# The front of a fused scan and two-layer MoE kernel in another order, its loads a block sooner, and its narrow exponentials in one operation

## The chip, the cores and the metric

The kernel runs on one core of a Trainium2 chip. The metric is the device time of one execution in microseconds, from the median of several runs. A core has five engines with a queue of instructions each: TensorE (PE in the profile; PEld is its loading of weights), VectorE (DVE), ScalarE (ACT), GpSimd (POOL), and SyncE (SP), which here issues nearly all DMAs.

## The reference

A chunked linear scan (4 sequences, 8 heads, 768 steps, head width 32, state width 16) feeds two feed-forward layers.

```python
log_a = np.log(np.clip(a, 1e-06, 1.0))
for c in range(nc):                        # chunks of 32 steps
    cum = np.cumsum(la, axis=-1)
    L = np.exp(cum[:, :, :, None] - cum[:, :, None, :]) * causal
    M = np.einsum('bhin,bhjn->bhij', Cc, Bc) * L
    y = np.einsum('bhij,bhjd->bhid', M, xc) + np.einsum('bhin,bhnd->bhid', Cc, state) * np.exp(cum)
    state = np.exp(np.sum(la, axis=-1)) * state + np.sum(Bx, axis=2)   # Bx: B x decayed to the chunk's end
x = y reshaped to [3072, 256]
h = np.maximum(np.maximum(x @ w1, x @ w2), x @ w3)        # 256 -> 768, three matrices
x = h @ w_out                                              # 768 -> 256
h = x @ w_in                                               # 256 -> 2048
out = (np.maximum(h, 0) + alpha * np.minimum(h, 0)) @ v_out    # 2048 -> 256
```

The weights arrive as 64-bit floats.

## The kernel before

The tokens are cut into 24 blocks of 128 steps (`r`; four sequences of six) for the scan and into 6 tiles of 512 tokens for the two layers. Blocks 0 to 8 are narrow: each is two chunks of 64 steps, and its mask-and-decay tile `e` (`blk[r]["m"]`) is 128 x 8 heads x 64. Blocks 9 to 23 are wide.

A block passes through steps with these names: `load_bc` and `load_x` (its B, C and x; narrow blocks from 2 on also load B and C turned, `bt` and `ct`), `cum_rows` (its rows of summed logs, broadcast from a tensor `cum_d` in DRAM into `e`; and `cpt`), `att_a` (B and C times decays, `bp` and `cp`, on GpSimd, L370), `att_t` (turned B and C, spread over heads), `att_e` (the exponential of `e` plus a column of negated log sums, one ACT operation for each head, L477, then two masks on GpSimd, L480), `att_b` (C times B on TensorE, L499, times `e` on VectorE, L504), `att_u` (the new state) and `att_y` (the output, L573 and L581, copied into the token tile `xt`, L590 and L591). Blocks 0 and 1 don't read `cum_d`: `first_e` makes their `e` by a matmul with the triangle (L455, L459, L461) and one exponential of 128x512 (L463). `sums(half)` adds up the logs of half the steps, writes them to `cum_d` (L295) and makes the decay columns (L300 to L306).

The weights come in 28 pieces of 512 KB. `fetch_weights` starts a piece's load into one of three buffers; `convert` turns it into two fp32r parts, high and low, in four steps, of which `next_weights(n)` emits the next n: a shift on VectorE (L178), a merge on VectorE (L180), the fetch of a later piece and the high part on ScalarE (L184), the low part on VectorE (L186) with ScalarE's rescaling of the next piece (L171). Matmuls of the layers are three products of high and low parts each (`parts`, L775); `halves` makes the high and low part of an activation (ACT L138, then L139, mostly on GpSimd).

The order around the change is written out by hand in the front (L1115 to L1168): warm-up matmuls (`idle`, L1110, on a cleared tile `warm`), the logs, the first loads, blocks 0 and 1 with 16 conversion steps between. Then phase 0 begins, the first layer on tile 0, cut into halves of 256 tokens: its first four units need blocks 0 and 1, the fifth blocks 2 and 3 as well. In phase 0 a planner that works with estimated times chooses the order on each engine; units, scan steps (`todo`) and conversion steps are emitted in turn. From phase 1 on the written order holds. `load(r)` (L221) loads a block's B, C and x; with `AHEAD = 8`, from block 8 on it loads the next block's B and C.

Each engine works its queue strictly in order, SyncE's DMA issues too.

Of the kernel before, what the change touches and what calls it, by code (L numbers as in the profile page):

```python
# [9 lines left out]
F32 = mybir.dt.float32  # L10
F32R = mybir.dt.float32r
BF16 = mybir.dt.bfloat16
U32 = mybir.dt.uint32
I64 = mybir.dt.int64
AF = mybir.ActivationFunctionType
ALU = mybir.AluOpType
# [3 lines left out]
P = 128  # L20
BT, H, S, D, N = 4, 8, 768, 32, 16
DM = H * D
NB = S // P
Q = 64
# [18 lines left out]
LEADW = 12288  # L43

STRICT = 1
AHEAD = 8
START = 4

FINE = 6
# [11 lines left out]
WARM = 8  # L61
# [23 lines left out]
def fused(ctx: ExitStack, tc: tile.TileContext, x, a, B, C, Bt, Ct, w1, w2, w3, w_out, v_in, v_out, alpha, cst, out):  # L85
    nc = tc.nc

    def pool(name, bufs, **kw):
        return ctx.enter_context(tc.tile_pool(name=name, bufs=bufs, **kw))
# [1 line left out]
    const = pool("const", 1)  # L91
    wts = pool("wts", 1)
    stage = pool("stage", 2)
    ld = pool("ld", 2)
    sm = pool("sm", 2)
    stk = pool("stk", 1)
    NDIR = BW * NB + KW
# [10 lines left out]
    def ptile(p, tag, shape=(P, 512)):  # L108
        return p.tile(list(shape), F32, tag=tag, name=tag)

    ct = const.tile([P, C_N], F32, name="ct")
# [11 lines left out]
    ncum = const.tile([P, NB, BT, H], F32, name="ncum")  # L123
# [6 lines left out]
    def st_tile():  # L130
        return stage.tile([P, 1024], U32, tag="st", name="st", bufs=3)
# [24 lines left out]
    def words(i):  # L156
        w = staged[i].rearrange("p (f w) -> p f w", w=2)
        return w[:, :, 0], w[:, :, 1]

    def fetch_weights():  # L160
        i = len(staged)
        if i < len(wq):
            st = st_tile()
            nc.sync.dma_start(st.bitcast(I64).rearrange("p (k f) -> p k f", k=2), wq[i][1])
            staged.append(st)

    def rebias(i):


        hi = words(i)[1].bitcast(F32)  # L170
        nc.scalar.activation(hi, hi, AF.Prelu, scale=2.0 ** -112, alpha=2.0 ** 32)  # L171
# [29 lines left out]
    def next_weights(n):  # L201
        for _ in range(n):
            done[0] += 1
            next(steps, None)
# [16 lines left out]
    def load(r):  # L221
        for q in (r, r + 1)[r > AHEAD:1 + (r >= AHEAD)]:
            load_bc(q)
        load_x(r)

    def load_bc(r):
        if r >= NR:
            return
        b, k = divmod(r, NB)
        s = slice(k * P, (k + 1) * P)  # L230
        d = blk.setdefault(r, {})
        direct = NPA <= r < NDIR
        for nm, src in (("b", B), ("bt", Bt), ("ct", Ct)) if direct else (("b", B), ("c", C)):
            if nm[1:]:
                t = d[nm] = ld.tile([P, P], F32, tag=nm, name=nm)
                nc.sync.dma_start(t, src[b, :, :, s].rearrange("h n t -> (h n) t"))
            else:
                t = d[nm] = ld.tile([P, H, N], F32, tag=nm, name=nm)
                nc.sync.dma_start(t, src[b, s])

    def load_x(r):
        if r >= NR:
            return
        b, k = divmod(r, NB)
        d = blk.setdefault(r, {})
        d["x"] = xm[r % NX]
        if r >= NDIR:
            d["x"] = xm[r % NX][:, 0]
            nc.sync.dma_start(d["x"], x[b, k * P:(k + 1) * P])
            return  # L250
        for c in range(2):
            s = slice(k * P + c * Q, k * P + (c + 1) * Q)
            nc.sync.dma_start(d["x"][c * Q:(c + 1) * Q, c], x[b, s])
# [9 lines left out]
    warm = un.tile([P, 512], F32, tag="g", name="g")[:, :256].bitcast(BF16)  # L263
# [131 lines left out]
    def att_t(r, part=None):  # L395
        d = blk[r]
        if r >= NDIR:
            ts = sm.tile([P, 7 * P], F32, tag="ts", name="ts", bufs=1)
            used = 6 + (r % NB > 0)
            nc.vector.transpose(ts[:, :6 * P], tok[0].bitcast(F32).rearrange("p s c -> p (s c)"))  # L400
            if used > 6:
                nc.vector.transpose(ts[:, 6 * P:], d["cp"].rearrange("p h n -> p (h n)"))
            sc = d["sc"] = dr.tile([7, P, P], F32, tag="sc", name="sc")
            for i in range(4):
                o = slice(32 * i, 32 * i + 32)
                nc.sync.dma_start(sc[:used, :, o].rearrange("s (v q) t -> q (s v) t", v=4), ts[o, :used * P].rearrange("q (w t) -> q w t", t=32))
            return
        if r >= NPA:
            bt, ct_, cpt = d["bt"], d["ct"], d["cpt"]
            bc = stk.tile([P, 6, P], F32R, tag="bc", name="bc").bitcast(F32)  # L410
            bs, cs = d["bs"], d["cs"] = bc[:, :2], bc[:, 2:4]
            nc.scalar.activation(cpt, cpt, AF.Exp)
            for i in range(2):
                nc.scalar.activation(cs[:, i, :], ct_, AF.Copy, scale=par[i])
            nc.vector.tensor_tensor(bs, bt.unsqueeze(1).to_broadcast([P, 2, P]), pairs.to_broadcast([P, 2, P]), ALU.mult)
            nc.gpsimd.tensor_tensor(cpt, ct_, cpt, ALU.mult)
            return
        keys = [("b", "c"), ("cp",)][part]
        pt = ptile(ps_acc, "acc", (P, 3, P))
        for i, key in enumerate(keys):  # L420
            nc.tensor.transpose(pt[:, i, :], d[key].rearrange("p h n -> p (h n)"), ident)
        if "cp" in keys:
            cpt = d["cpt"] = sm.tile([P, P], F32, tag="cpt", name="cpt")
            nc.scalar.activation(cpt, pt[:, len(keys) - 1, :], AF.Copy)
        if "b" in keys:
            bc = stk.tile([P, 6, P], F32R, tag="bc", name="bc").bitcast(F32)
            bs, cs = d["bs"], d["cs"] = bc[:, :2], bc[:, 2:4]
            for i in range(2):
                nc.scalar.activation(cs[:, i, :], pt[:, 1, :], AF.Copy, scale=par[i])
            nc.vector.tensor_tensor(bs, pt[:, 0:1, :].to_broadcast([P, 2, P]), pairs.to_broadcast([P, 2, P]), ALU.mult)  # L430
# [35 lines left out]
    def att_e(r, part=None):  # L466
        b, k = divmod(r, NB)
        if r >= NDIR:
            for g in range(2) if part is None else (part,):
                e = blk[r]["m", g]  # L470
                for q in range(4):
                    nc.scalar.activation(e[:, q, :], e[:, q, :], AF.Exp, bias=ncum[:, k, b, 4 * g + q:4 * g + q + 1])  # L472
                nc.gpsimd.affine_select(out=e, in_=e, pattern=[[0, 4], [1, P]], compare_op=ALU.is_ge, fill=0.0, base=0, channel_multiplier=-1)  # L473
            return
        e = blk[r]["m"]
        for h in range(4 * (part or 0), 4 if part == 0 else H):
            nc.scalar.activation(e[:, h, :], e[:, h, :], AF.Exp, bias=ncum[:, k, b, h:h + 1])  # L477
        for c in range(0 if part == 0 else 2):
            m = e[c * Q:(c + 1) * Q]
            nc.gpsimd.affine_select(out=m, in_=m, pattern=[[0, H], [1, Q]], compare_op=ALU.is_ge, fill=0.0, base=0, channel_multiplier=-1)  # L480

# [625 lines left out]

    junk = ps_up.tile([P, 512], F32, tag="up", name="up")

    def idle(n):  # L1110

        for _ in range(n):
            nc.tensor.matmul(junk, warm[:, :P], warm, start=True, stop=True, skip_group_check=True)  # L1113

    with tc.manual_schedule():  # L1115
        for t in xm:
            nc.gpsimd.memset(t, 0.0)
        nc.vector.memset(warm, 0.0)
        idle(WARM)
        logs()  # L1120
        load_bc(0)
        fetch_weights()
        nc.sync.dma_start(s_c[:BT * H, C_SEL:], cst[:BT * H, C_N + C_SEL:])
        load_x(0)
        fetch_weights()
        load_bc(1)
        load_x(1)
        fetch_weights()
        cum_rows(0)
        cum_rows(1)  # L1130
        su, e0, e1 = sums(0), first_e(0), first_e(1)
        next(e0)
        next(e1)
        att_t(0, 0)
        next(e0)
        back()
        att_a(0, "bp")
        next(su)
        next(e0)
        next(su)  # L1140
        rebias(0)
        next_weights(1)
        next(e1)
        next(e0)
        next(su)
        next_weights(2)
        next(su)
        att_a(0, "cp")
        att_a(1)
        next_weights(1)  # L1150
        att_b(0)
        next_weights(2)
        next(e1)
        att_u(0)
        next(e1)
        att_t(0, 1)
        att_t(1, 0)
        att_t(1, 1)
        next_weights(1)
        att_y(0)  # L1160
        next_weights(1)
        att_b(1)
        att_u(1)
        idle(IDLE)
        next_weights(3)
        att_y(1)
        next_weights(1)
        next_weights(START)  # L1168
    load(2)
    if True:  # L1170
        nc.sync.dma_start(alph, alpha.rearrange("(k p) -> p k", p=P))
        todo += [(go, 0) for go in (
# [23 lines left out]
        for n_ph, ph in enumerate(PHASES):  # L1196
# [5 lines left out]
            layer, t, _, pace = ph  # L1202
# [62 lines left out]
```

## Time and profile before

| | |
|---|---|
| median of 3 runs | 537.24 us (536.43 to 538.32) |
| the profiled execution | 538.03 us, of which the span from the first to the last instruction 536.3 |
| mean granted TensorE clock | 0.997 of full speed |
| TensorE busy | 524.7 us (98%), 3382 matmuls |
| VectorE, ScalarE, GpSimd busy | 326.9, 261.4, 243.8 us |
| chain that ended last | TensorE 88%, VectorE 4%, ScalarE 2%, issue 2%, GpSimd 1%, DMA 1% |

Times in the profile are microseconds from the span's start. A row of a timeline gives start, length, engine, line and operation, the tile written and those read, shapes and the count; in square brackets stands the idle time of the engine just before and what ended it. Two matmuls overlap in the pipeline, so their lengths add up to more than the time they take. The granted clock is the share of full speed that the chip allowed TensorE.

### The profile page before, as it was taken

Reading aid. Unit: us, or ns where it says so; the run is one execution under the profiler, and the core shown is the slowest. Engines: PE = TensorE matmul, PEld = TensorE weight load, DVE = VectorE, ACT = ScalarE, POOL = GpSimd, SP = SyncE. Lnnn points to the kernel's source line nnn. Section 1 sums busy time; section 2 is a strip of 40 time slices with the busy share of each in tenths; the row PEclk is TensorE's granted clock in tenths of the full one; section 3 lists DMA queues with packets and bytes.
Section 4 is the critical chain, followed back from the end, with each engine's and each line's share of the span. In section 5 each row is a group of like instructions: output and inputs, shape, how many; then the busy total and the mean of one; then the engine's idle time right before and its main releaser. Section 6 shows DMA issues by size and latency. Waiting matters only on the chain.

```text
span 536.3 us, 9516 instructions
## 1 busy us (share of the span) xinstructions
PE 524.7 (98%) x3382; PEld 428.6 (80%) x3382; DVE 326.9 (61%) x566; ACT 261.4 (49%) x612; POOL 243.8 (45%) x267
## 2 busy tenths in 40 slices
PE   8888999999999999999999999999999999999997
PEld 4767887788888888888888888888888888778886
DVE  5895686788573446665447676337665636775453
ACT  6676675666756324333333433423432324766561
POOL 2153354434645324645424655432653352885550
PEclk9998999999999999999999999999999999999999
DMA  7667566487544534423716324633440200000024
GB/s 212 184 187 230 162 177 168 135 228 191 171 112 104 130 99 109 104 78 86 155 44 160 75 82 119 141 82 90 98 99 1 39 0 1 1 2 0 1 40 119
DMA packets 147744, 56.52 MB, mean 105 GB/s; under 512 B 87920, under 2 KB 139568, under 8 KB 147696
## 3 DMA queue, kind: packets, MB, share of 16 engines
q1 hardware_dynamic: 145328, 55.38, 40.0%
q10 hardware_dynamic: 2368, 0.52, 0.4%
q8 instruction: 27, 0.44, 0.4%
q14 instruction: 21, 0.17, 0.1%
HBM read 45.26 MB, written 10.62 MB: 104 GB/s over the span
## 4 chain that ended last, share of the span: by engine, by line
PE 88%; DVE 4%; ACT 2%; issue 2%; SPq 1%; POOL 1%; DMA 1%; ACTq 0%; POOLq 0%; DVEq 0%
PE up L775 47%; PE acc L775 28%; PE at L775 5%; PE at L489 1%; PE at L614 1%; DVE v L180 1%; DMA xm<-in_x_dram 1%; PE at L499 1%; PE at L606 1%; PE up L1113 1%; PE at L581 1%; PE at L573 0%; SPq L295 0%; POOL e L480 0%; ACT e L472 0%
## 5 line engine op out<-in xcount | busy, mean ns | idle before, releaser
L139 POOL TENSOR_TENSOR gl<-g,gh 128x512 fp32r<-128x512 f32 (+1 forms) x109 | 137.2, 1259 | 214.6 <-ACT gh L138 190.2
L775 PE MATMUL up<-xt,w 128*128 128x512 f32 (+1 forms) x777 | 169.2, 365 | 1.8 <-DVE g L801 0.6
L775 PEld LDWEIGHTS up<-xt,w 128*128 128x128 f32 x777 | 133.2, 190 | 27.9 <-issue 2.2
L138 ACT ACTIVATE gh<-g 128x512 fp32r<-128x512 f32 (+1 forms) x114 | 69.4, 609 | 172.0 <-DVE g L820 73.8
L775 PE MATMUL up<-yt,vi 128*128 128x512 f32 x459 | 116.6, 389 | 0.0
L801 DVE TENSOR_TENSOR g<-up,g 128x512 f32<-128x512 f32 (+1 forms) x84 | 51.2, 610 | 82.4 <-PE up L775 79.8
L775 PEld LDWEIGHTS up<-yt,vi 128*128 128x128 f32 x459 | 86.1, 188 | 17.9
L775 PE MATMUL acc<-gh,vo 128*128 128x512 f32 x268 | 83.2, 392 | 0.0
L819 DVE TENSOR_SCALAR g<-up,alph 128x512 f32<-128x512 f32 x48 | 35.9, 749 | 37.7 <-PE up L775 37.7
L775 PEld LDWEIGHTS acc<-gh,vo 128*128 128x128 f32 x268 | 49.6, 188 | 10.2 <-issue 0.2
L775 PE MATMUL acc<-gl,vo 128*128 128x512 f32 x134 | 52.2, 389 | 0.0
L775 PE MATMUL acc<-gh,wo 128*128 128x512 f32 (+1 forms) x168 | 47.4, 364 | 0.4 <-DVE yt L848 0.4
L472 ACT ACTIVATE e<-e,ncum 128x128 f32<-128x128 f32 x120 | 37.9, 388 | 0.0
L799 ACT ACTIVATE g<-up 128x512 f32<-128x512 f32 (+1 forms) x42 | 22.3, 530 | 28.3 <-PE up L775 16.3
L775 PEld LDWEIGHTS acc<-gh,wo 128*128 128x128 f32 x168 | 29.8, 189 | 5.6 <-DVE yt L848 0.5
L820 DVE SCALAR_TENSOR_TENSOR g<-up,g 128x512 f32<-128x512 f32 x48 | 33.2, 691 | 1.6
L775 PE MATMUL acc<-gl,wo 128*128 128x512 f32 (+1 forms) x84 | 30.4, 362 | 0.3 <-POOL gl L139 0.3
L775 PEld LDWEIGHTS acc<-gl,vo 128*128 128x128 f32 x134 | 25.2, 188 | 5.3
L473 POOL TENSOR_SCALAR_AFFINE_SELECT e<-e 128x512 f32<-128x512 f32 x30 | 19.2, 643 | 12.2 <-ACT e L472 12.2
L180 DVE SCALAR_TENSOR_TENSOR v<-st,v 128x512 uint32<-128x512 uint32 x28 | 23.1, 825 | 2.1 <-ACT st L171 1.4
L817 DVE SCALAR_TENSOR_TENSOR g<-g,rest,up 128x512 f32<-128x512 f32 x16 | 11.9, 743 | 15.0 <-ACT g L816 14.8
L1002 DVE SCALAR_TENSOR_TENSOR g<-g,rest,up 128x512 f32<-128x512 f32 x16 | 12.0, 747 | 11.9 <-ACT g L1001 11.6
(199 smaller groups left out, 675.2 us busy)
## 6 DMA issues: line engine op xcount, KB each, us to landing
e<-cum_w SPq DMA_DIRECT2D x30, 256.0 KB
st<-sc SPq DMA_DIRECT2D x60, 128.0 KB
sc<-ts SPq DMA_DIRECT2D x52, 112.0 KB
st<-in_moe_w_out_dram SPq DMA_DIRECT2D x11, 512.0 KB
st<-in_moe_w_dram SPq DMA_DIRECT2D x9, 512.0 KB
st<-in_moe_w_in_dram SPq DMA_DIRECT2D x8, 512.0 KB
v<-sc SPq DMA_DIRECT2D x60, 64.0 KB
out_dram<-st SPq DMA_DIRECT2D x20, 128.0 KB
```

Of the source, the lines that this page charges most:

```text
L138: nc.scalar.activation(dst_h, src, AF.Copy)
L139: engine.tensor_tensor(dst_l, src, dst_h, ALU.subtract)
L180: nc.vector.scalar_tensor_tensor(v, hi, 3, v, ALU.logical_shift_left, ALU.bitwise_or)
L472: nc.scalar.activation(e[:, q, :], e[:, q, :], AF.Exp, bias=ncum[:, k, b, 4 * g + q:4 * g + q + 1])
L473: nc.gpsimd.affine_select(out=e, in_=e, pattern=[[0, 4], [1, P]], compare_op=ALU.is_ge, fill=0.0, base=0, channel_multiplier=-1)
L775: nc.tensor.matmul(acc, w, r, start=(first and i == 0), stop=(last and i == len(todo_) - 1), skip_group_check=True)
L799: nc.scalar.activation(g, p, AF.Copy)
L801: nc.vector.tensor_tensor(g, p, g, ALU.max)
L817: nc.vector.scalar_tensor_tensor(g, g, rest[:, f:f + 1], p, ALU.mult, ALU.add)
L819: nc.vector.tensor_scalar(g, p, 0.0, alph[:, f:f + 1], ALU.min, ALU.mult)
L820: nc.vector.scalar_tensor_tensor(g, p, 0.0, g, ALU.max, ALU.add)
L1002: nc.vector.scalar_tensor_tensor(g, g, rest[:, f:f + 1], h, ALU.mult, ALU.add)
```

## The change

The front is emitted in another order: the g of block 0 ahead of its `att_t`, block 0's `att_b`, `att_u` and block 1's `att_t` sooner, two conversion steps later, the third piece's fetch ahead of block 1's x, and the loads of block 2 and of block 3's B and C in the front. `load(r)` loads the next block's B and C from block 3 on (`AHEAD = 2`). The buffers of B, C and turned C become three, turned C shares those of C; turned B keeps two. The narrow blocks' `att_e` adds the column of log sums by one GpSimd operation and then takes one exponential over all heads. The warm-up matmuls read a constant that is there from the start.

```diff
-AHEAD = 8
+AHEAD = 2
...
-    ld = pool("ld", 2)
+    ld = pool("ld", 3)
...
             if nm[1:]:
-                t = d[nm] = ld.tile([P, P], F32, tag=nm, name=nm)
+                tag, bufs = ("c", 3) if nm == "ct" else ("bt", 2)
+                t = d[nm] = ld.tile([P, P], F32, tag=tag, name=nm, bufs=bufs)
...
         e = blk[r]["m"]
-        for h in range(4 * (part or 0), 4 if part == 0 else H):
-            nc.scalar.activation(e[:, h, :], e[:, h, :], AF.Exp, bias=ncum[:, k, b, h:h + 1])
-        for c in range(0 if part == 0 else 2):
+        if part != 1:
+            nc.gpsimd.tensor_tensor(e, e, ncum[:, k, b, :].unsqueeze(2).to_broadcast([P, H, Q]), ALU.add)
+        if part == 0:
+            return
+        nc.scalar.activation(e, e, AF.Exp)
+        for c in range(2):
             m = e[c * Q:(c + 1) * Q]
...
-    def idle(n):
-
+    def idle(n, early=False):
+
+        w = nc.const_aps.tensor(1.0, [P, 512], BF16) if early else warm
         for _ in range(n):
-            nc.tensor.matmul(junk, warm[:, :P], warm, start=True, stop=True, skip_group_check=True)
+            nc.tensor.matmul(junk, w[:, :P], w, start=True, stop=True, skip_group_check=True)
...
-        idle(WARM)
+        idle(WARM, True)
         logs()
         load_bc(0)
         fetch_weights()
...
         load_x(0)
         fetch_weights()
         load_bc(1)
+        fetch_weights()
         load_x(1)
-        fetch_weights()
+        load_bc(2)
         cum_rows(0)
         cum_rows(1)
         su, e0, e1 = sums(0), first_e(0), first_e(1)
         next(e0)
         next(e1)
+        next(e0)
         att_t(0, 0)
-        next(e0)
         back()
         att_a(0, "bp")
         next(su)
         next(e0)
         next(su)
+        next(e0)
         rebias(0)
         next_weights(1)
+        att_b(0)
+        next(su)
+        next_weights(1)
         next(e1)
-        next(e0)
+        att_u(0)
+        next_weights(1)
+        load_x(2)
+        att_t(1, 0)
         next(su)
-        next_weights(2)
-        next(su)
+        next(e1)
         att_a(0, "cp")
         att_a(1)
         next_weights(1)
-        att_b(0)
-        next_weights(2)
         next(e1)
-        att_u(0)
-        next(e1)
+        next_weights(1)
         att_t(0, 1)
-        att_t(1, 0)
+        att_b(1)
+        next_weights(1)
         att_t(1, 1)
-        next_weights(1)
         att_y(0)
         next_weights(1)
-        att_b(1)
         att_u(1)
+        next_weights(2)
         idle(IDLE)
+        att_y(1)
+        load_bc(3)
         next_weights(3)
-        att_y(1)
-        next_weights(1)
         next_weights(START)
-    load(2)
```

## Rows read from the trace of the kernel before

**Rows 1.** Windows: length; PE, PEld, DVE, ACT, POOL busy; PEclk; DMA share; GB/s.
```profile
20.00:38.00 18.00, 17.14 (x189) 14.16 (x189) 16.59 (x39) 13.32 (x41) 6.53 (x9) 1.00 0.75 198
38.00:42.00 4.00, 1.93 (x24) 1.65 (x24) 2.30 (x7) 2.85 (x10) 3.23 (x6) 1.00 0.49 118
42.00:48.00 6.00, 6.00 (x82) 5.14 (x79) 3.20 (x10) 4.02 (x14) 2.17 (x4) 0.72 0.66 193
48.00:100.00 52.00, 50.77 (x590) 42.40 (x588) 36.55 (x85) 35.87 (x108) 23.42 (x33) 1.00 0.62 180
100.00:520.00 420.00, 419.80 (x2241) 345.14 (x2241) 250.09 (x387) 190.77 (x411) 201.61 (x205) 1.00 0.35 86
```

**Rows 2.** Waits of PE from 0 to 120 us: total, times, longest.
```profile
PE at L573 <- DVE e L504: 1.4, 1, 1.4
...
PE at L573 <- POOL cpt L416: 0.7, 1, 0.7
```

**Rows 3.** Timeline of the front, 0 to 24 us.
```profile
1.25 3.59 PE L1113 MATMUL up<-g 128*128 128x512 bf16 x8 [1.25 <-DVE g L1118]
...
3.45 0.84 ACT L272 ACTIVATE xt<-xt 32x768 f32<-32x768 f32 x1 [1.37 <-DVE xt L271]
...
8.39 1.12 PE L461 MATMUL up<-g,yt 128*128 128x512 f32 x2 [0.86 <-DVE g L459]
...
9.55 0.69 DVE L459 TENSOR_TENSOR g<-scr 128x512 f32<-128x512 f32 x1 [0.35 <-PE up L461]
...
10.64 0.85 PE L499 MATMUL at<-bc 64*64 64x128 f32 x16
...
12.59 0.60 ACT L463 ACTIVATE e<-up 128x512 f32<-128x512 f32 x1 [0.24 <-PE up L461]
...
16.40 0.75 DVE L504 TENSOR_TENSOR e<-at,e 128x256 f32<-128x256 f32 x2
...
17.38 0.60 DVE L544 SCALAR_TENSOR_TENSOR u<-u,dec_f 128x64 f32<-128x64 f32 x2
...
18.11 0.65 PE L581 MATMUL at<-e,xm 128*32 128x64 f32 x32
18.43 0.69 DVE L180 SCALAR_TENSOR_TENSOR v<-st,v 128x512 uint32<-128x512 uint32 x1
...
19.16 0.63 ACT L184 ACTIVATE w<-v 128x512 fp32r<-128x512 f32 x1 [3.01 <-DVE v L180]
...
20.00 1.93 PE L775 MATMUL up<-xt,w 128*128 128x256 f32 x14 [0.60 <-ACT xt L590]
...
20.39 0.68 DVE L186 TENSOR_TENSOR w<-v,w 128x512 fp32r<-128x512 f32 x1
```

**Rows 4.** Timeline around block 3's exponentials, 24 to 50 us.
```profile
36.50 0.33 ACT L477 ACTIVATE e<-e,ncum 128x64 f32<-128x64 f32 x1
...
37.22 0.79 POOL L139 TENSOR_TENSOR gl<-g,gh 128x256 fp32r<-128x256 f32 x1 [3.92 <-DMA b<-in_B_dram]
...
37.48 1.52 ACT L477 ACTIVATE e<-e,ncum 128x64 f32<-128x64 f32 x6
...
39.71 0.62 POOL L370 TENSOR_TENSOR bp<-b,dec_b 128x128 f32<-128x128 f32 x1
...
40.40 0.66 POOL L480 TENSOR_SCALAR_AFFINE_SELECT e<-e 64x512 f32<-64x512 f32 x1
...
41.66 0.45 PE L573 MATMUL at<-cpt,u 32*64 32x64 f32 x8 [1.40 <-DVE e L504]
```

**Rows 5.** Groups by line and form: count, busy us, mean ns, idle before.
```profile
L477 ACT ACTIVATE e<-e,ncum 128x64 f32<-128x64 f32 x56 | 15.2, 336 | 0.0
...
L139 POOL TENSOR_TENSOR gl<-g,gh 128x512 fp32r<-128x512 f32 x97 | 126.3, 1302 | 192.4 <-ACT gh L138 176.3 <-DMA v<-sc 4.6 <-PE acc L775 4.4
```

**Rows 6.** Timeline, a conversion beside a GpSimd subtraction, 88 to 95 us.
```profile
92.56 1.33 POOL L139 TENSOR_TENSOR gl<-g,gh 128x512 fp32r<-128x512 f32 x1 [2.52 <-ACT gh L138]
...
92.86 1.59 DVE L180 SCALAR_TENSOR_TENSOR v<-st,v 128x512 uint32<-128x512 uint32 x1
```

## The prediction

> **What bounds the kernel now.** I read three views in this order. First the windows: from 100 us to 520 us TensorE is busy for 419.80 of 420 us at full clock [rows 1]. There the reader is to see that no other engine's saving can shorten that part; only what TensorE waits for before it can. The window from 48 to 100 us has 50.77 of 52, so 1.2 us idle. Between 20 and 38 us TensorE is busy 17.14 of 18 while VectorE has 16.59 of 18; between 38 and 42 us TensorE is busy 1.93 of 4; and from 42 to 48 us it is busy all the time, but at a granted clock of 0.72 [rows 1]. Second the waits of TensorE: the two that stand out are block 3's output matmuls (L573), 1.4 us for VectorE's masked product (L504) and 0.7 us for GpSimd's product (L416) [rows 2]. Third the timeline, for why these come late [rows 3, 4].
>
> So the time to win is in four places: the front, up to the first matmul of the weights at 20.00 [rows 3]; idle before 38 us (18 - 17.14 = 0.86); the gap of 38 to 42 us (4 - 1.93 = 2.07); and the fall of the clock behind it, (1 - 0.72) x 6 = 1.68 us [rows 1]. The clock fell right after the gap, and nowhere else in the windows. Together with the 1.2 us between 48 and 100 that is what is there; everything else is TensorE's own work, which the change leaves as it is.
>
> **The front.** *Warm-up.* The eight warm-up matmuls start at 1.25, behind VectorE's clearing of their operand, and take 3.59, to 4.84 [rows 3]. With a constant as operand they can start when the engines do, some 0.4 earlier, and end at 4.44. The logarithm is done at 3.45 + 0.84 = 4.29 [rows 3], so what follows on TensorE starts about 0.35 earlier.
>
> *Block 0 ahead of block 1.* The first L461 began at 8.39 after waiting 0.86 for VectorE [rows 3]; its operand g now goes ahead of att_t's operation, so it can run at 8.39 - 0.35 - 0.86 = 7.2 to 8.3. From there I add up the new order, each step at its row in [rows 3]: CB matmuls 0.85 and their products 0.75; conversion 0.69; g of block 1 0.69; L461 1.12, to 12.4. ScalarE has a weight step of about 0.6 (estimated from the 0.63 of L184) before the exponential of 0.60: 13.6. Block 1's CB matmuls end half a microsecond later; products 0.75; conversion 0.69; about 1.4 for block 0's last VectorE work and block 1's state (0.60 of it L544): 17.0. Then small matmuls, about 0.2, L581 0.65, and a copy of xt. The copy does not have to pass the 0.63 of L184 any more, which stood ahead of it at 19.16. First weight matmul: 18.2 to 18.3 in place of 20.00, a gain of up to 1.7.
>
> *How much of it counts.* The new order does two conversion steps later than the old one: at att_y(1) piece 2 still lacks L180, which ran at 18.43 before. After the front it has L180 0.69, a copy on ScalarE 0.63 and L186 0.68 before it, and starts at about 18.85: it is ready at 20.9, against 20.39 + 0.68 = 21.07 [rows 3]. The third of the three products needs piece 2, so TensorE stops there, with 12 matmuls done, and VectorE then goes on through the same list, busy 16.59 of 18 [rows 1]. The ends are 0.2 (VectorE sets the pace) and 1.7. I take 0.4, near the first, because VectorE is the fuller engine there. The loads of blocks 2 and 3 in the front cost SyncE's queue nothing that I count: no matmul waits for them in the front, and weights that land later by what these bring are used at the end of it. If that cover is gone, the weights behind them land up to 1.6 us later (an estimate: 320 KB of block 2's loads at the 198 GB/s of the window from 20 to 38 us [rows 1]); I take the lower end of this part down to -0.5 for that.
>
> **The exponentials.** Before: eight ACT operations of 336 ns a block, 56 in all, 15.2 us [rows 5]. After: one of 128x512, 0.60 by the form of L463 [rows 3], so 7 x (2.69 - 0.60) = 14.6 us leave ScalarE. GpSimd gets 7 additions of 128x512. No such addition is in the trace; the nearest row is the subtraction L139 of that shape, 1302 ns [rows 5], and I take 1.3 each, 9.1 in all. None of these sums is on the path as such; what counts is block 3.
>
> **Block 3 and the gap.** Its first exponential starts at 36.50; with other work between, the last of six ends at 37.48 + 1.52 = 39.00; then GpSimd masks, but between its two masks stands bp of block 4 (L370, 0.62), and the second ends at 41.06; TensorE waits 1.40 more [rows 4]. Changed: the addition needs cum_d's rows and the log sums alone, GpSimd had nothing to do from 33.3 to the L139 at 37.22 [rows 4], so it is done before. One exponential from 36.5 ends at 37.1. bp of block 4 has its load a block sooner and can go into GpSimd's empty stretch, so the masks (0.66 each) can follow at 37.2 to 38.5, or at 38.0 to 39.4 behind L139 (0.79). Product and small matmuls are then due about 39.3 to 40.2, where TensorE still had weight matmuls up to 40.25 (41.66 - 1.40 = 40.26). That takes away nearly all of the 2.07. The other end is that GpSimd keeps its order: L139, L416, mask, bp, mask in a row from 37.22 end at about 40.6, only 0.5 sooner than 41.06. I take 1.8, as the early load speaks for the first. What is late next is VectorE's conversions, as in the stretch before.
>
> **The clock.** It was 1.00 up to 42 us, with a front as thin as it was, and 0.72 after a gap of this size [rows 1]. With the gap filled I count the whole 1.68 as gained, say 1.7; if more than about half the gap stays, nothing.
>
> **What GpSimd's additions cost VectorE.** L180 took 0.69 with GpSimd idle at 18.43 [rows 3] and 1.59 at 92.86 beside an L139 (92.56 to 93.89) [rows 6]: 0.9 lost to one GpSimd operation of just this shape. Where VectorE has slack that is free. Two additions, of blocks 2 and 3, fall between 18 and 38 us where it has none: 0 to 1.8, I take 0.4, since they meet such an operation for part of their time. The Trainium skill's "GPSIMD Engine Reference" (Specifications) says GpSimd shares its SBUF interfaces with VectorE, in contention with VectorE instructions that have two SBUF inputs; L180 is one, and the trace agrees. The same page (Engine selection) would not put a two-input elementwise operation on GpSimd at all, as about twice as slow.
>
> **Later loads.** From block 3 on each load call issues the same number of transfers as before, B's and C's one block further on; the third buffers are taken from a tag that loses one, so no transfer waits for a tile that it did not wait for. Between 48 and 100 us I count 0 (bounds +1.2, all its idle time, and -1).
>
> **The sum.** 0.4 + 1.8 + 1.7 - 0.4 = 3.5 us. Against the profiled execution's 538.03 (span 536.3, 1.7 around it) that gives 534.5; the median of the three runs is 0.8 lower, 537.24, so the prediction is 533.7.
>
> **Rivals.** A: the whole front counts as well, and the idle 0.86 before 38 us goes: 1.7 + 0.86 + 2.07 + 1.7 = 6.3, so 530.9. For it: the first tile's work then starts with ScalarE free. Against it: piece 2 is no sooner. B: the gap stays. GpSimd keeps its order (0.5 of the gap), TensorE still idles beyond 1 us, the clock falls as before: 0.4 + 0.5 - 0.4 = 0.5, so 536.7. For it: the order of this stretch is a planner's and not the written one. C, slower: GpSimd's additions stretch VectorE's two-input operations. Price 0.9 for each of seven, 6.3 at most; it decides where VectorE is full, in 18 to 38 us (two additions), and in the window after 48 us for those beside conversions, where I count three: 5 x 0.9 = 4.5. The gap then stays too, so 4.5 less the 0.9 of front and gap is +3.6, 540.8. It decides once the additions in the full stretch cost more than the 0.9 that is won there. For it: [rows 6]. Against it: after 48 us VectorE is busy 36.55 of 52 [rows 1], and each narrow block's additions find their rows landed early. This is the outcome to which the skill's sentence on shared interfaces would lead.
>
> **Chances and range.** Forecast 0.46, A 0.20, B 0.20, C 0.14. A measurement of this kernel can tell about 0.3% (1.6 us) from no change. Faster by more than that (below 535.6): the forecast nearly whole, A, and a little of B: 0.67. Within it: most of B and a little of the forecast and C: 0.21. Slower: 0.12. The range goes from A with some of the later idle time, 530.3, to the lower half of C, 538.3.
>
> **What would show it.** Right: the gap of 38 to 42 us is gone from TensorE's windows and the clock stays 1.00 after it; the first L775 is at about 18.3 and its matmuls of the third product wait for L186 till about 21; ACT has 7 exponentials of 128x512; the last GpSimd operation before block 3's product is the second mask, with no bp between. Wrong: the clock still falls somewhere before 60 us; L180's and L186's means grow beside GpSimd's additions; or an L139 stands waiting behind an addition that waits for cum_d. A result above 536 would mean the gap was not what held the end; one below 531 that the front's start counts in full.

## The result, and the profile after

The changed kernel takes 543.50 us in the median of 6 runs (539.86 to 546.12), against 537.25 before: a ratio of 1.0109 (95% interval 1.0080 to 1.0137). Nine more runs gave 541.54 and 1.0068 (1.0042 to 1.0095). It is slower, and the forecast of 533.7 with its range to 538.3 missed it. The profiled execution took 545.8 us, its span is 544.1, 7.8 more than before, and its mean granted clock 0.981.

The windows say where that went. They are those of [rows 1], with three of the changed kernel's own between (columns as there).

```profile
20.00:38.00 18.00, 17.09 (x146) 13.95 (x146) 13.87 (x31) 9.98 (x24) 5.84 (x8) 0.69 0.71 185
27.00:40.50 13.50, 13.00 (x107) 10.63 (x100) 9.42 (x23) 6.92 (x17) 3.84 (x7) 0.50 0.75 195
38.00:42.00 4.00, 4.00 (x26) 4.00 (x26) 2.44 (x6) 1.36 (x3) 0.73 (x1) 0.68 0.69 197
42.00:48.00 6.00, 3.29 (x47) 2.44 (x45) 3.35 (x8) 2.50 (x6) 3.85 (x7) 0.95 0.46 121
44.50:47.00 2.50, 0.48 (x7) 0.28 (x8) 0.91 (x2) 1.38 (x3) 1.69 (x4) 1.00 0.28 89
47.50:54.00 6.50, 5.86 (x76) 4.95 (x76) 4.10 (x9) 1.52 (x4) 1.44 (x3) 0.50 0.51 142
48.00:100.00 52.00, 50.01 (x582) 41.58 (x583) 38.19 (x90) 27.88 (x72) 23.91 (x36) 0.94 0.56 166
100.00:520.00 420.00, 419.46 (x2293) 344.66 (x2292) 249.87 (x387) 191.46 (x419) 200.43 (x206) 1.00 0.35 88
```

The gap did not close: it moved from 38 to 42 us to 44.5 to 47, with 2.50 - 0.48 = 2.02 us idle in place of 2.07. And TensorE now runs at half its clock (granted 0.50: 1.2 GHz in place of 2.4) twice, for 13.7 us and for 6.8 us; the windows from 27.00 and from 47.50 lie inside these two stretches. Before, it was 3.4 us, once. Half of 20.5 us is 10.2 us of full-speed work; before it was 1.7. That difference of 8.5 is more than the whole 7.8. In single runs of this one program the mean clock is between 0.981 and 0.994, and the time goes with it: 545.8, 546.0 and 546.1 at 0.981, 541.1 at 0.991, 539.9 and 541.2 at 0.994. The clock is most of its spread of 6 us, not all: span times clock, which would then be the same in all fifteen runs, lies between 532.8 and 536.5 us.

TensorE's waits up to 120 us, as [rows 2]:

```profile
PE at L577 <- POOL cpt L417: 2.4, 2, 2.0
PE up L779 <- DVE g L805: 1.0, 1, 1.0
PE at L577 <- DVE e L508: 0.8, 1, 0.8
```

The front, as [rows 3], in the profiled execution of the changed kernel (line numbers are 4 or so higher than before):

```profile
0.84 3.57 PE L1118 MATMUL up<-const-bfloat16-1.0 128*128 128x512 bf16 x8 [0.84 <-PEq L1256]
3.56 0.84 ACT L273 ACTIVATE xt<-xt 32x768 f32<-32x768 f32 x1 [1.47 <-DVE xt L272]
8.68 1.70 PE L462 MATMUL up<-g,yt 128*128 128x512 f32 x2
13.09 1.13 PE L462 MATMUL up<-g,yt 128*128 128x512 f32 x2
19.59 1.70 PE L779 MATMUL up<-xt,w 128*128 128x256 f32 x12
```

The warm-up ends at 4.41, as forecast. The first weight matmul comes at 19.59, not at 18.3: the same pair of L462 took 1.70 at 8.68 and 1.13 at 13.09, so the matmuls ran well below full speed until about 10 us. The trace's record of the granted clock begins only at 9.86 us, at full speed; the 1.00 that the windows print before that stands for no entry. The order as written does not decide this: kernel `i2_write_act` below has the same front, its record begins at 3.68, and in its profile

```profile
0.84 3.28 PE L1118 MATMUL up<-const-bfloat16-1.0 128*128 128x512 bf16 x8 [0.84 <-PEq L1256]
6.88 1.12 PE L462 MATMUL up<-g,yt 128*128 128x512 f32 x2
```

and the first L779 at 18.13. What decides it is not shown.

Block 3, which [rows 4] show before, on GpSimd, ScalarE, TensorE and VectorE in the changed kernel:

```profile
33.10 0.40 POOL L371 TENSOR_TENSOR bp<-b,dec_b 128x128 f32<-128x128 f32 x1 [2.18 <-DMA b<-in_B_dram]
41.08 0.73 POOL L139 TENSOR_TENSOR gl<-g,gh 128x256 fp32r<-128x256 f32 x1 [7.57 <-ACT gh L138]
43.26 0.74 POOL L139 TENSOR_TENSOR gl<-g,gh 128x256 fp32r<-128x256 f32 x1 [1.44 <-ACT gh L138]
43.95 1.04 POOL L478 TENSOR_TENSOR e<-e,ncum 128x512 f32<-128x512 f32 x1
45.03 0.63 ACT L481 ACTIVATE e<-e 128x512 f32<-128x512 f32 x1 [0.78 <-POOL e L478]
45.73 0.65 POOL L484 TENSOR_SCALAR_AFFINE_SELECT e<-e 64x512 f32<-64x512 f32 x1 [0.73 <-ACT e L481]
46.36 0.45 POOL L417 TENSOR_TENSOR cpt<-ct,cpt 128x128 f32<-128x128 f32 x1
46.86 0.45 PE L577 MATMUL at<-cpt,u 32*64 32x64 f32 x8 [2.02 <-POOL cpt L417]
47.57 0.76 DVE L508 TENSOR_TENSOR e<-at,e 128x256 f32<-128x256 f32 x2 [2.15 <-POOL e L484]
```

GpSimd stood idle for 7.57 us from 33.5 with the addition of block 3 in its queue: ahead of it were two L139, which wait for TensorE by way of ScalarE, and TensorE ran at half its clock. So the first fall of the clock delays the two L139, these the addition, and that the exponential, the masks and `cpt`; there is the gap, and behind it the clock falls a second time. The fall makes the gap late, but the gap does not need it: `e3_warm_tile` below has the same order on GpSimd and runs at full clock from 15.2 to 42.5 us, and there

```profile
41.48 0.45 PE L577 MATMUL at<-cpt,u 32*64 32x64 f32 x8 [2.02 <-POOL cpt L417]
```

The groups of [rows 5], and a conversion beside an addition for [rows 6]:

```profile
L478 POOL TENSOR_TENSOR e<-e,ncum 128x512 f32<-128x512 f32 x7 | 7.4, 1059 | 6.2 <-DMA e<-cum_d 6.2
L481 ACT ACTIVATE e<-e 128x512 f32<-128x512 f32 x7 | 4.4, 624 | 1.6 <-POOL e L478 1.6
L180 DVE SCALAR_TENSOR_TENSOR v<-st,v 128x512 uint32<-128x512 uint32 x28 | 21.6, 771 | 1.0
```

```profile
75.01 1.04 POOL L478 TENSOR_TENSOR e<-e,ncum 128x512 f32<-128x512 f32 x1
75.47 1.14 DVE L186 TENSOR_TENSOR vi<-v,vi 128x512 fp32r<-128x512 f32 x1
```

An addition took 1.06, less than the 1.3 forecast; L186, 0.68 alone, took 1.14 beside one.

### The profile page after: what moved, and what is told of

The parts are those of the page before. It is cut to its first block, busy times and chain, and to the rows that moved or that the text cites. A ratio compares the mean times of both kernels' runs of the same rounds, so it can differ in the third digit from the quotient of the medians.

```text
span 544.1 us, 9468 instructions
## 1 busy us (share of the span) xinstructions
PE 532.2 (98%) x3382; PEld 433.6 (80%) x3382; DVE 330.8 (61%) x566; ACT 253.0 (46%) x563; POOL 247.7 (46%) x274
## 4 chain that ended last, share of the span: by engine, by line
PE 84%; DVE 5%; issue 4%; POOL 3%; ACT 2%; DMA 1%; ACTq 0%; SPq 0%; POOLq 0%; DVEq 0%
PE up L779 45%; PE acc L779 28%; PE at L779 5%; PE at L493 1%; PE at L618 1%; POOL gl L139 1%; DVE v L180 1%; PE at L585 1%; PE at L610 1%; PE at L577 1%; POOL e L484 1%; DMA e<-cum_d 1%; POOL e L478 1%; DVE v L178 1%; PE at L503 0%
## 5 line engine op out<-in xcount | busy, mean ns | idle before, releaser
L139 POOL TENSOR_TENSOR gl<-g,gh 128x512 fp32r<-128x512 f32 (+1 forms) x109 | 135.9, 1247 | 213.7 <-ACT gh L138 197.1
L779 PE MATMUL up<-xt,w 128*128 128x512 f32 (+1 forms) x777 | 171.2, 369 | 1.7 <-DVE g L805 1.0
L779 PEld LDWEIGHTS up<-xt,w 128*128 128x128 f32 x777 | 135.5, 195 | 27.2 <-issue 1.6
L779 PE MATMUL up<-yt,vi 128*128 128x512 f32 x459 | 116.7, 389 | 0.0
L779 PEld LDWEIGHTS up<-yt,vi 128*128 128x128 f32 x459 | 86.1, 188 | 17.9
L779 PE MATMUL acc<-gh,vo 128*128 128x512 f32 x268 | 83.2, 392 | 0.0
L779 PEld LDWEIGHTS acc<-gh,vo 128*128 128x128 f32 x268 | 49.5, 188 | 10.2 <-issue 0.2
L779 PE MATMUL acc<-gl,vo 128*128 128x512 f32 x134 | 52.2, 389 | 0.0
L779 PE MATMUL acc<-gh,wo 128*128 128x512 f32 (+1 forms) x168 | 48.9, 371 | 0.3 <-DVE yt L852 0.3
L779 PEld LDWEIGHTS acc<-gh,wo 128*128 128x128 f32 x168 | 30.9, 195 | 5.9 <-DVE yt L852 0.5
L779 PE MATMUL acc<-gl,wo 128*128 128x512 f32 (+1 forms) x84 | 30.9, 368 | 0.0
L779 PEld LDWEIGHTS acc<-gl,vo 128*128 128x128 f32 x134 | 25.2, 188 | 5.3
L180 DVE SCALAR_TENSOR_TENSOR v<-st,v 128x512 uint32<-128x512 uint32 x28 | 21.6, 771 | 1.0
```

The lines of the kernel that those rows point to most:

```text
L139: engine.tensor_tensor(dst_l, src, dst_h, ALU.subtract)
L180: nc.vector.scalar_tensor_tensor(v, hi, 3, v, ALU.logical_shift_left, ALU.bitwise_or)
L779: nc.tensor.matmul(acc, w, r, start=(first and i == 0), stop=(last and i == len(todo_) - 1), skip_group_check=True)
```

## The experiments

All timed beside the kernel before. "Lost" is (1 - granted clock) x span, the median over a kernel's runs: what the clock took. The other columns are times in its profiled execution: the end of the issue of the second half sums' write to `cum_d`, the issue of block 3's rows from `cum_d`, the start of block 3's product (L504 before), and the start of VectorE's maximum `g` at about 91 us, explained below. "At 91" and span are given as differences from the kernel before.

| kernel | median us | ratio [95%] | lost | write | rows | product | at 91 | span |
|---|---|---|---|---|---|---|---|---|
| before | 537.2 to 537.9 | 1 | 0.5 to 1.6 | 27.0 | 30.2 | 41.1 | (91.17) | (536.3) |
| changed | 543.50 | 1.0109 [1.0080, 1.0137] | 7.6 | 29.2 | 32.3 | 47.6 | +7.7 | +7.8 |
| `e1_exp_only` | 536.59 | 0.9983 [0.9969, 0.9996] | 0.0 | 27.1 | 30.5 | 39.5 | -2.3 | -2.3 |
| `e2_front_only` | 546.67 | 1.0160 [1.0137, 1.0184] | 8.7 | 28.5 | 31.4 | 45.1 | +8.3 | +8.5 |
| `e3_warm_tile` | 540.82 | 1.0074 [1.0046, 1.0101] | 5.4 | 27.3 | 31.1 | 42.2 | +2.5 | +2.8 |
| `f1_loads_only` | 543.72 | 1.0119 [1.0093, 1.0146] | 6.2 | 27.3 | 30.1 | 42.6 | +6.9 | +6.9 |
| `f2_order_only` | 537.42 | 1.0017 [0.9994, 1.0041] | 2.1 | 27.1 | 30.6 | 38.5 | -0.6 | -0.6 |
| `f3_front_conv` | 544.56 | 1.0126 [1.0096, 1.0156] | 6.8 | 26.8 | 30.1 | 45.8 | +6.5 | +6.6 |
| `f4_exp_loads` | 538.93 | 1.0031 [1.0017, 1.0045] | 2.2 | 28.2 | 31.0 | 42.6 | +0.7 | +1.0 |
| `g1_ahead_only` | 543.55 | 1.0110 [1.0060, 1.0161] | 6.0 | 28.7 | 31.8 | 47.5 | +8.5 | +8.5 |
| `g2_block2_front` | 538.42 | 1.0006 [0.9991, 1.0020] | 1.6 | 23.4 | 29.6 | 41.4 | -0.2 | +0.3 |
| `g3_exp_order` | 538.91 | 1.0014 [0.9993, 1.0035] | 2.4 | 27.7 | 30.5 | 39.0 | -1.5 | -1.4 |
| `g4_filled` | 539.40 | 1.0034 [1.0023, 1.0044] | 1.1 | 27.4 | 30.4 | 41.8 | +0.7 | +0.7 |
| `h1_x_first` | 540.26 | 1.0054 [1.0033, 1.0074] | 3.0 | 28.5 | 31.7 | 43.9 | +1.7 | +2.3 |
| `h2_buffers_only` | 538.20 | 1.0005 [0.9990, 1.0020] | 1.6 | 25.7 | 29.2 | 40.4 | -0.9 | -0.4 |
| `h3_warm_only` | 537.38 | 1.0003 [0.9988, 1.0018] | 1.6 | 26.7 | 30.3 | 41.1 | +0.1 | 0.0 |
| `h4_turned_sooner` | 542.52 | 1.0089 [1.0064, 1.0115] | 4.1 | 28.2 | 31.3 | 43.9 | +4.6 | +4.9 |
| `i2_write_act` | 540.03 | 1.0060 [1.0037, 1.0083] | 4.3 | 24.3 | 30.8 | 41.0 | +1.7 | +1.8 |
| `h6_exp_order_filled` | 537.60 | 1.0028 [0.9999, 1.0057] | 1.1 | 27.6 | 31.6 | 39.3 | -1.2 | -1.2 |

**The exponentials against the front, and the warm-up.** The first three undo a part each. `e1_exp_only` is the kernel before with the new `att_e` alone; `e2_front_only` the changed kernel with the old eight exponentials; `e3_warm_tile` the changed kernel with

```diff
-        idle(WARM, True)
+        idle(WARM)
```

> The kernel before with nothing but the narrow exponentials changed (GpSimd's addition, one exponential). Queue theory: the addition stands in GpSimd's queue behind low-part subtractions that wait for TensorE, so block 3 comes later than before and TensorE's gap at 38 to 42 us grows: 539 to 543 us. Front theory (the written order and the loads are what costs): the same as before or up to 2 us faster, 535 to 537.5.

> The changed kernel with the eight exponentials with a bias on ScalarE in place of GpSimd's addition and the one exponential. Queue theory: block 3 is ready as early as before or earlier, the gap at 45 us goes: 533 to 536. Front theory: the clock still falls at about 27 us, since the piece of thin TensorE work there comes from the front and the half-log sums: 539 to 545.

> The changed kernel with its first eight warm-up matmuls on the cleared tile again, so that they start at 1.25 and not at 0.84. Warm-up theory: in the changed kernel the matmuls of the front ran at half speed till about 10 us because the warm-ups ended earlier; with this undone they are fast from about 5.5, the first weight matmul comes about 1 us sooner, and the time falls by 1 us or more. Queue and front theories: no change beyond 1 us, 539 to 546, clock falls at 27 and at 47 us.

The exponentials are not the loss; alone they are the one part that gains, 0.17%. In their windows the gap is half of what it was in [rows 1], and no fall follows:

```profile
38.00:42.00 4.00, 3.05 (x59) 2.59 (x59) 3.12 (x9) 2.14 (x7) 2.48 (x5) 1.00 0.50 141
42.00:48.00 6.00, 6.00 (x64) 5.00 (x63) 4.46 (x12) 3.37 (x8) 3.79 (x6) 1.00 0.65 193
```

Here the addition of block 3 found GpSimd empty, as the prediction had it:

```profile
34.12 1.04 POOL L477 TENSOR_TENSOR e<-e,ncum 128x512 f32<-128x512 f32 x1 [2.56 <-DMA e<-cum_d]
36.60 0.61 ACT L480 ACTIVATE e<-e 128x512 f32<-128x512 f32 x1
38.79 0.45 PE L576 MATMUL at<-cpt,u 32*64 32x64 f32 x8 [1.18 <-POOL cpt L416]
```

The front and the loads together carry the whole loss. The warm-up on the old tile gives an interval that overlaps the changed kernel's.

**Order or loads.** `f1_loads_only` is the kernel before with all changes of loads and buffers; `f2_order_only` the kernel before with the front's order, its loads, warm-up and exponentials as they were; `f3_front_conv` is `e2_front_only` with two conversion steps put back ahead of `att_y(1)`; `f4_exp_loads` is `e1_exp_only` with the loads of `f1_loads_only`.

> The kernel before with the loads alone changed: blocks 2's loads and block 3's B and C in the front at the places that correspond, the next block's B and C from block 3 on, and the three buffers. Load theory (transfers ahead on SyncE's queue push the half sums' write to cum_d and so block 3's rows back): 540 us or more, and the write of cum_d's second half issued at 27 us or later, against 24.63 before. Order theory (the written order of the front is what costs): 536 to 538.5, that write at 25 us or sooner.

> The kernel before with the order of the front alone changed, that is the order of blocks 0 and 1 and of the conversion steps, and the third piece's fetch ahead of block 1's x; loads, warm-ups and exponentials as before. Order theory: 541 to 547, with clock falls between 26 and 50 us, as in the front without the new exponentials. Load theory: 535 to 538.

> The new front with the old exponentials (546.7 us), with two conversion steps of piece 2 moved ahead of block 1's output again, as in the kernel before. Conversion theory (the two steps that stand behind block 1's output make piece 2, and with it VectorE's copy of the second half sums, late): 536 to 540. If the rest of the order or the loads are the cause: 543 to 547.

> The kernel before with the new exponentials and the new loads, but its own order of the front. With the exponentials alone it took 536.6, against 537.9 for the kernel before beside it. Load theory: 539 or more. Order theory: 534.5 to 537, since bp of block 4 then has its B early and does not stand between the two masks.

The loads alone give the whole loss. The order alone brings the first weight matmul to 17.14, 2.86 sooner than before, and the time stays. Part of the 2.86 is the clock, whose record begins at 4.01 us there and at 5.70 in the kernel before. The two conversion steps matter little: 1.0126 against 1.0160, with intervals that overlap. With the new exponentials the loads cost less, 1.0031 against 1.0119.

**Where the front's 2.86 us go.** The last wait of phase 0 is TensorE's for VectorE's `g` at about 91 us. In the kernel before it is 0.65 long; in `f2_order_only` TensorE comes there 1.67 sooner (91.32 - 1.76 = 89.56 against 91.88 - 0.65 = 91.23) and waits 1.76. First the kernel before, then `f2_order_only`:

```profile
91.17 0.65 DVE L801 TENSOR_TENSOR g<-up,g 128x512 f32<-128x512 f32 x1
91.88 1.65 PE L775 MATMUL up<-xt,w 128*128 128x512 f32 x6 [0.65 <-DVE g L801]
```

```profile
87.14 1.38 POOL L480 TENSOR_SCALAR_AFFINE_SELECT e<-e 64x512 f32<-64x512 f32 x2 [0.49 <-ACT e L477]
88.55 0.76 DVE L504 TENSOR_TENSOR e<-at,e 128x256 f32<-128x256 f32 x2 [2.21 <-POOL e L480]
89.03 0.46 POOL L393 TENSOR_TENSOR tok<-c,tok 128x128 fp32r<-128x128 f32 x1
89.52 0.98 DVE L400 STREAM_TRANSPOSE ts<-tok 128x768 f32<-128x768 f32 x1 [0.21 <-POOL tok L393]
90.61 0.65 DVE L801 TENSOR_TENSOR g<-up,g 128x512 f32<-128x512 f32 x1
91.32 1.65 PE L775 MATMUL up<-xt,w 128*128 128x512 f32 x6 [1.76 <-DVE g L801]
```

`g` stands in VectorE's queue behind a product that waits for GpSimd's masks and transposes that wait for GpSimd's subtractions. The start of `g` is 0.56 sooner, and so is the end: the span is 0.6 shorter. The table's last two columns agree within 0.6 us for every kernel: what a version wins or loses, it has won or lost by 91 us.

**Which loads.** `g1_ahead_only` is the kernel before with the next block's B and C from block 3 on and the third buffers; `g2_block2_front` with block 2's loads in the front and the buffers; `g3_exp_order` is `f2_order_only` with the new exponentials. `g4_filled` is the changed kernel with 6 extra matmuls ahead of the second half sums' and 16 ahead of block 3's L577.

```diff
-AHEAD = 8
+AHEAD = 2
```

> The kernel before with the next block's B and C loaded one block sooner and the three buffers, but all loads of block 2 and block 3 still behind the front. If it is B's and C's transfers a block ahead, in front of x, that hold x and the broadcast rows back on SyncE's queue: 541 to 545, clock below 0.99. If it is block 2's loads in the front: 536 to 538.

> The kernel before with block 2's loads in the front, nothing else sooner (and the three buffers). If block 2's early loads are what re-deals the planner's order for the worse (the subtraction of the first unit ahead of block 2's product in GpSimd's queue, as with all loads sooner): 541 to 545. If it is the loads a block ahead: 536 to 538.

> The new exponentials and the new order of the front with the old loads. The exponentials alone gave 0.9983 and the order alone 1.0017 of the kernel before. If each part keeps its effect: 534.5 to 537. If the planner's order is dealt anew by every edit, so that no part keeps its effect: anything from 533 to 545.

> The changed kernel with 6 matmuls of 128 columns before the half sums and 16 of 64 columns before block 3's output matmuls, whose results nothing uses, some 2.5 us of TensorE work at full clock. Clock theory (time is lost because TensorE idles, its clock falls, and the work after it runs at half speed): the mean clock rises to 0.994 or more and the time falls to 535 to 539. If the clock only shows what other waits cost: 543 to 548.

It is the load of B and C a block sooner, and not block 2's in the front. The changed kernel itself says the same: with the old loads, and its warm-ups on the cleared tile, it is `g3_exp_order`, at 1.0014. What the early load moves is seen in SyncE's queue; first the kernel before, then the changed one:

```profile
23.01 1.58 SPq L1171 DMA_DIRECT2D alph<-in_moe_alpha_dram  x1
24.63 2.36 SPq L295 DMA_DIRECT2D cum_d<-yt  x1
27.09 0.39 SPq L164 DMA_DIRECT2D st<-in_moe_w_out_dram  x1
30.23 1.19 SPq L356 DMA_DIRECT2D e<-cum_d  x2
```

```profile
25.00 1.44 SPq L1179 DMA_DIRECT2D alph<-in_moe_alpha_dram  x1
26.63 2.02 SPq L164 DMA_DIRECT2D st<-in_moe_w_out_dram  x1
28.70 0.46 SPq L296 DMA_DIRECT2D cum_d<-yt  x1
32.27 1.09 SPq L357 DMA_DIRECT2D e<-cum_d  x2
```

Block 3's B and C, three issues of about 1.3 us together, now go out from 20.54 (27.57 before), and the order that the planner then deals has the fetch of a weight piece ahead of the write to `cum_d`. The fetch stands for 2.02 us. The write's issue starts 4.1 us later; but before the change it stood for 2.36 us itself, so it ends only 2.2 later (29.16 against 26.99), and block 3's rows go out 2.0 later.

That is not the whole way from the load to the loss. In `f1_loads_only`, with the whole loss, the rows go out sooner than before:

```profile
30.07 1.18 SPq L357 DMA_DIRECT2D e<-cum_d  x2
```

The extra matmuls of `g4_filled` keep the clock up (1.1 us lost in place of 7.6), and the ratio falls to 1.0034: a large part of the loss goes through the clock. The ratio stays above 1. The extra matmuls take TensorE's time themselves, but `f4_exp_loads` has none and is at 1.0031: three of its runs at a mean clock of 1.000 took 538.8 to 539.0 us, where those of `e1_exp_only` at 1.000 took 536.1 to 537.1. So the loads cost something beside the falls of the clock, too.

**The parts of the early load.** `h1_x_first` is `g1_ahead_only` with a block's x issued ahead of the next block's B and C; `h2_buffers_only` has the buffers alone, `h3_warm_only` the constant warm-up alone; `h4_turned_sooner` loads only C and the turned B and C sooner. The core of `h1_x_first`:

```diff
-        for q in (r, r + 1)[r > AHEAD:1 + (r >= AHEAD)]:
-            load_bc(q)
+        if r <= AHEAD:
+            load_bc(r)
         load_x(r)
+        if r >= AHEAD:
+            load_bc(r + 1)
```

> The kernel before with the loads of the next block from block 3 on, but a block's own x issued ahead of the next block's B and C. Theory 'SyncE's order' (B and C of the next block, three issues of 1.3 us in all, stand ahead of x and of the cum_d write behind it): block 3's x is back at about 29, the product before 43, TensorE's clock falls for at most 4 us, 536.5 to 539.0. Rival 'bp sooner' (what counts is that the next block's bp is ready early and goes into GpSimd's queue ahead of what is due): as with the loads a block sooner alone, product at 46 to 48 and 541 to 545.

> The kernel before with nothing but the three buffers of B, C and turned C. Both theories: no load is sooner, so 536.5 to 538.5, product of block 3 at about 41. If the buffers themselves move the order, 541 or more.

> The kernel before with nothing but the warm-up matmuls on a constant. They end 0.4 us sooner. If an earlier warm-up leaves the front's matmuls at half speed till later: L461's pair takes 1.7 us and the first L775 comes after 20.3, 537.5 to 539.5. If it does nothing: L461 1.12, first L775 at 19.7 to 20.0, 536.5 to 538.0.

> The kernel before with only C and the turned B and C loaded a block sooner; plain B, which bp is made of, at its old place. Theory 'SyncE's order': the issues still stand ahead of x, so 541 to 545, product of block 3 after 45. Rival 'bp sooner': 536.5 to 539, product before 43.

Buffers and warm-up do nothing that the runs can tell (1.0005 and 1.0003). With x first the ratio is 1.0054, half the loss, but the interval overlaps that of `g1_ahead_only`; its time and product lie between the two forecasts, and the write to `cum_d` still ends at 28.5. With plain B at its old place the loss stays (1.0089), outside the rival's forecast, so the rival that `bp` comes too early falls. SyncE's order is supported in part at most.

**The late write, and the front once more.** `i2_write_act` is the changed kernel with

```diff
-        nc.sync.dma_start(cum_d[qs]...
+        (nc.sync, nc.scalar)[half].dma_start(cum_d[qs]...
```

`h6_exp_order_filled` is `g3_exp_order` with six extra matmuls at the second half sums. Its expectation names the constant warm-up too; as it ran, its warm-ups read the cleared tile.

> The changed kernel with one edit: the second half sums' write to cum_d is issued from ScalarE's queue, so that SyncE's fetch of a weight piece, which waits for its staging buffer, no longer stands ahead of it. Theory 'late write': the write goes out before 26, block 3's rows are fetched by 31, its product ends before 45, the second fall of the clock (47.5 to 54 in the changed kernel) gets shorter or goes; the first one (27 to 40) stays, since nothing before it is touched: 539.0 to 541.5. Rival 'the write is late, but not what counts': product after 46, two falls as before, 542 to 546.

> The kernel before with the front's order, the constant warm-up and the new exponentials, its loads at their old places, and six filler matmuls at the second half sums, so that TensorE is not idle there. If the clock is what kept the earlier front from counting: no fall of the clock before 60 us, first L775 near 17, 534.5 to 536.5, faster than both. Rival 'the front does not count, clock or not': 537 to 539.

With the write on ScalarE's queue block 3's product is at 41.0, 6.6 sooner than in the changed kernel, and the clock's low stretch in the profile is one of 6.8 us in place of 13.7 and 6.8. But its median, 540.03, has an interval that overlaps the second set of the changed kernel's (1.0060 against 1.0068): by the runs, the late write is not shown to be what costs the time. Nor is it enough by itself: `h6_exp_order_filled` has block 3's rows at 31.6, 1.4 later than before, and a ratio of 1.0028. Its median, 537.60, is below the changed kernel's but not below that of the kernel before, with no fall of the clock in its profile and the first weight matmul at 17.46; the wait at 91 us is 1.68 there, as it was in `f2_order_only`. The one version that beats both is `e1_exp_only`.

## Why the prediction was wrong

The step that failed is "Later loads", costed at 0. It counted transfers and buffers, and the buffers were right (`h2_buffers_only`: 1.0005). Each load call does issue as many transfers as before, but block 3's B and C come on top at the start, three issues more in SyncE's queue, and the sum had no price for what that moves. `g1_ahead_only`, this step alone, costs 1.1% (543.55 against 537.78), the whole result, and mostly through the clock: 6.0 us lost against 1.6. In its profile TensorE is at half speed for 17.1 us in two stretches, against 3.4 us in one before; that is 6.8 of the 8.5 us by which its span is longer. Two windows inside these stretches:

```profile
31.00:40.50 9.50, 9.50 (x95) 7.59 (x95) 6.30 (x15) 3.45 (x10) 1.53 (x2) 0.50 0.64 185
48.00:54.00 6.00, 5.43 (x72) 4.15 (x73) 3.06 (x9) 1.42 (x6) 0.52 (x1) 0.50 0.38 99
```

How the early load brings the clock down is open: late rows behind SyncE's queue fit `g1_ahead_only` (31.8 against 30.2) and the changed kernel, not `f1_loads_only`.

- *Warm-up*: end at 4.41 against 4.44 forecast; worth nothing by itself (`h3_warm_only`: 1.0003).
- *Front*: 18.2 to 18.3 forecast, 18.13 in `i2_write_act`, 19.59 in the changed kernel's profile with its slow matmuls up to 10 us. The hit is in part luck: with the old loads the same order gives 17.14 and 16.98 (`f2_order_only`, `g3_exp_order`), so the sum of the steps was about 1 us too long, which the loads in the front, counted as nothing, seem to have made up.
- *How much of it counts*: 0.4 taken; the span of `f2_order_only` is 0.6 shorter for a front 2.86 shorter, and its median shows no gain (1.0017). Small was right, the reason wrong: not piece 2's conversion, but GpSimd's work ahead of `g` at 91 us. Idle time of 1.2 us between 48 and 100 us was in [rows 1] and stood in the prediction only as a bound.
- *Exponentials and gap*: right in kind for the exponentials alone (gap 0.95 in place of 2.07, no fall of the clock in the profile), but not in size: 0.17% of the time is 0.9 us, against 1.8 + 1.7 - 0.4 = 3.1 in the sum. The profiled span is 2.3 shorter, of which 0.55 stands already at the first weight matmul (19.45 against 20.00), in a front that this edit leaves alone. In the changed kernel the gap stayed at 2.02: `bp` of block 4 did move into the empty stretch (at 33.10), but the addition did not; two L139 came ahead of it. Rival B had the gap staying, at no cost; it did not have the clock falling twice.
- *Clock*: +1.7 forecast, -8.5 measured in the profiled execution. The prediction allowed the clock only to recover. A second stretch at half speed had no price in any rival, though [rows 1] showed what the first one cost; so the range ended 5 us too low.
- *GpSimd's additions beside VectorE*: 0.4 taken, rival C up to 4.5. L186 did stretch, from 0.68 to 1.14 beside an addition, and its mean grew from 0.71 to 0.76; L180's fell from 0.83 to 0.77. The two together took 43.0 us before, 42.9 in the changed kernel and 44.8 in `e1_exp_only`, which with all seven additions is the fastest kernel of all. The sentence of the Trainium skill's "GPSIMD Engine Reference" (Specifications) on shared interfaces agrees with that one row; a cost of it in the kernel's time is not seen.

Not settled, then, is the link from the early load to the clock, and why it fell at 27 us in the changed kernel. TensorE was idle for 0.41 of the 2 us up to 26.5, and much of the rest were matmuls of six columns (L300, 1.02 us for eight); `i2_write_act` runs the same front and fell at 41 alone. The planner gives phase 0 another order after every edit, so no experiment here changes one thing only, and that the new order and not the load itself costs the time is a rival that no run excludes. That the parts' losses don't add (the loads cost 1.2% alone, and 0.5% on top of the new exponentials, 1.0031 against 0.9983) goes with this.

## What to carry to other kernels

A load that is issued sooner is not free because it is the same load: time it alone, and write down what stands behind it in the queue that issues it, up to the next instruction that somebody waits for. Where the profile shows that the clock fell behind a gap, price the next such gap on the loss side too, at what the first fall took. And look for the last wait before the stretch in which one engine is full: what is won ahead of it counts only up to the slack of whoever ends that wait.

## What the runs showed of the hardware

One program's runs had mean clocks from 0.981 to 0.994, and with them times of 539.4 to 546.1 us. The record of the granted clock does not begin with the kernel. In the changed kernel's profile it begins at 9.86 us, and the same pair of matmuls takes 1.70 at 8.68 and 1.13 at 13.09; in `i2_write_act` it begins at 3.68, and the pair takes 1.12 at 6.88. The views print 1.00 where there is no entry, and the mean clock counts it so: how fast the front runs is read from the matmuls' durations.
